# Turning v by VectorE in 32x32 blocks instead of by TensorE, in a channel attention with a gated convolution

## Chip, core and metric

The kernel runs on one core of a Trainium2 chip. The metric is the device time of one execution in microseconds (us); the median of the runs counts. The engines are TensorE (PE; PEld is its weight load), VectorE (DVE), ScalarE (ACT), GpSimd (POOL) and SyncE (SP). SP and ACT issue the transfers, which 16 DMA queues carry.

## The reference

Four batches (B = 4) of q, k, v with N = 6336 rows and C = 256 channels, float32. The attention is over channels: the scores are a 256x256 matrix, summed over all rows.

```python
qn = q / (np.linalg.norm(q, axis=1, keepdims=True) + 1e-06)
kn = k / (np.linalg.norm(k, axis=1, keepdims=True) + 1e-06)
s = kn.transpose(0, 2, 1) @ qn / tau
a = softmax(s, axis=-1)                  # 256 x 256 a batch
x = v @ a                                # 6336 x 256
gate_pre[t] = sum over k of conv_w[k] * x[t - 4 + k]   # 5 taps, causal, per channel
out = (sigmoid(gate_pre) * (x @ w_val)) @ w_out
```

## The kernel before

**Scores.** q and k come in groups of three rows a partition (`load_group`, tile `raw`, six buffers). `score_group` splits them into a high part in a reduced format (`hi`, ACT cast, L196) and the rest (POOL subtraction, L197), and TensorE adds three products of the parts into `s_ps` (L232). In the first batch most groups go in unsplit. For the norms ACT squares (`sq`, L213), and DVE and POOL add the squares (`acc_ps` and `acc`, L218).

**Softmax.** `softmax(b)` is a generator. Each `tick()` issues its next piece, between pieces of other work. At its end the batch has its weights `w` (a, and a times w_val, both split).

**The gated convolution.** The rows are cut into 13 chunks a batch: 12 of 508 rows and one of 240, each with a halo of 4 rows ahead of it. The products need v with channels on the partitions. So `load_v` brings a chunk with rows on the partitions (`v_raw`, three buffers), and `transpose_v` turns it: eight TensorE transposes of 128x128 a chunk into PSUM (`t_ps`, L359), an ACT cast to `v_hi` (L360), and a DVE subtraction to `v_lo` (L361), for each half of the channels. `product` makes x (`x_ps`) and x times w_val (`val_ps`) at L369, `conv` sums the five taps (ACT at L383, DVE at L385), `sigmoid`, `value` (DVE, L398) and `split_g` (`g_hi` on ACT, L411; `g_lo` on POOL, L412) follow, and `finish` multiplies by w_out (L428) and stores.

**The order.** The last loop runs over the 52 chunks of all batches. Chunk n's step holds sigmoid, value and split of n, the convolution of n + 1, the transposes of n + 2, the load of n + 3, the product with w_out of n - 1, and one or two groups of the next batch's scores, until they run out. In the first batch nothing but scores can run. A scheduler then places each instruction on its engine's queue by its own estimate of times. `behind(...)` adds that what follows is placed after a marked instruction. Each engine runs its queue in order.

Of the kernel before, what the change touches and what calls it, by code (L numbers as in the profile page):

```python
# [9 lines left out]
F32 = mybir.dt.float32  # L10
F32R = mybir.dt.float32r
# [3 lines left out]
ALU = mybir.AluOpType  # L15
# [3 lines left out]
P = 128  # L19
GROUP = 3  # L20
LEAD = 4
PREFETCH = 4
VLEAD = 2
SIDE, LAST = 5, 15
HALO = 4
ROWS = 508
# [3 lines left out]
def kernel(  # L30
# [13 lines left out]
    nc = tc.nc  # L44
    B, N, C = q.shape
    K = conv_w.shape[0]
    NH = C // P
# [4 lines left out]
    raw_p = ctx.enter_context(tc.tile_pool(name="raw_p", bufs=6))  # L52
# [4 lines left out]
    v_p = ctx.enter_context(tc.tile_pool(name="v_p", bufs=VLEAD + 1))  # L57
    w_p = ctx.enter_context(tc.tile_pool(name="w_p", bufs=2))
    ps_s = ctx.enter_context(tc.tile_pool(name="ps_s", bufs=1, space=PSUM))
    ps = ctx.enter_context(tc.tile_pool(name="ps", bufs=4, space=PSUM))  # L60
# [23 lines left out]
    ident = const.tile([P, P], F32, name="ident")  # L84
# [245 lines left out]
    NT = -(-(HALO + WMAX) // P)  # L330

    vraw, vt = {}, {}

    def load_v(b, i):

        t0, w = chunks[i]
        t = raw_p.tile([P, NT, C], F32, name="v_raw", bufs=3)
        j0 = 0
        if i == 0:
            nc.gpsimd.memset(t[0:HALO, 0, :], 0.0)  # L340
            nc.sync.dma_start(out=t[HALO:P, 0, :], in_=v[b, 0:P - HALO])
            j0 = 1
        full, rest = divmod(HALO + w, P)
        lo = t0 - HALO
        nc.sync.dma_start(out=t[:, j0:full, :], in_=v[b, lo + j0 * P:lo + full * P].rearrange("(j p) c -> p j c", p=P))
        if rest:
            nc.sync.dma_start(out=t[0:rest, full, :], in_=v[b, lo + full * P:t0 + w])
        vraw[b, i] = t

    def transpose_v(b, i, h):  # L350
        w = HALO + chunks[i][1]
        if h == 0:
            vt[b, i] = [v_p.tile([P, NH, HALO + WMAX], F32R, name=name) for name in ("v_hi", "v_lo")]
        th, tl = vt[b, i]
        src = vraw[b, i]
        tp = ps.tile([P, 512], F32, name="t_ps", tag="bank")
        for j in range(-(-w // P)):
            np_ = min(P, w - j * P)
            marks["PE"] = nc.tensor.transpose(tp[:, j * P:j * P + np_], src[0:np_, j, h * P:(h + 1) * P], ident[0:np_, 0:np_])  # L359
        nc.scalar.copy(th[:, h, 0:w], tp[:, 0:w])  # L360
        nc.vector.tensor_tensor(tl[:, h, 0:w], tp[:, 0:w], th[:, h, 0:w].bitcast(F32), ALU.subtract)  # L361

    def product(ps, wt, which, b, i, h, lo, hi_):
        th, tl = vt[b, i]
        hs = slice(h * P, (h + 1) * P)
        n_ = 0
        for ch in range(NH):
            for ws, vs in ((0, th), (0, tl), (1, th)):
                marks["PRODUCT"] = nc.tensor.matmul(ps, wt[:, which, ws, ch, hs], vs[:, ch, lo:hi_], start=n_ == 0, stop=n_ == 3 * NH - 1)  # L369
                n_ += 1  # L370
# [86 lines left out]
    @contextmanager  # L457
    def behind(*engines):
        with ExitStack() as st:
            for e in engines:  # L460
                st.enter_context(tc.issue_after(marks[e].ins))
            yield
# [34 lines left out]
    def step(n):  # L497
        return all_steps[n] if 0 <= n < len(all_steps) else None
# [24 lines left out]
        for _ in gen:  # L523
            pass
    tick()
    with tc.high_priority(), behind("PE", "ACT"):
        for h in range(NH):
            transpose_v(*step(0), h)
    with behind("PE", "ACT"):
        run_group()  # L530
    with behind("PE"):
# [16 lines left out]
    if WORDS == 2:  # L548
        with behind("ACT"):
            nc.scalar.copy(wo_hi.rearrange("p h e -> p (h e)"), w_raw["out"][:, :, 1].bitcast(F32))  # L550
    for h in range(NH):
        transpose_v(*step(1), h)
    with behind("ACT"):
        split_group()

# [6 lines left out]
    for n in range(len(all_steps)):  # L562
# [32 lines left out]
                with behind("ACT"):  # L595
                    split_group()
        if new:
            for h in range(NH):
                transpose_v(*new, h)
        tick()  # L600
        if prev:
            with behind(*{len(all_steps) - 2: ["CONV"], len(all_steps) - 1: ["G"]}.get(n, [])):
# [34 lines left out]
```

## Time and profile before

| | |
|---|---|
| median of 3 runs | 655.57 us (655.3 to 656.13) |
| profiled execution, span from first to last instruction | 653.5 us |
| mean granted TensorE clock | 0.998 |
| transposes `t_ps` on TensorE | 400 of 416 recorded, 54.2 us modelled busy time for the full ones |
| bytes from HBM, to HBM | 79.11 MB, 25.95 MB |

The span begins with the first instruction and ends with the last. The median is of executions without the profiler, which take a little more than the span from end to end. A row of the profile has line, engine, operation, tiles, shapes and count, then the busy time and the mean of one instruction, then the idle time ahead of them and what ended it.

### The profile page before, as it was taken

To read this page: it belongs to the slowest core of one execution; us is meant where nothing else is said; L and a number is where in the kernel's file an instruction comes from. 1 tells how busy PE (TensorE), PEld (TensorE's weight loads), DVE (VectorE), ACT (ScalarE), POOL (GpSimd) and SP (SyncE) were. 2 spreads that over 40 slices of the span, in tenths; PEclk is the share of its full clock that TensorE was granted. 3 is DMA by queue.
4 is the path that set the end of the run, shared out by engine and by line. 5 is a ranking of instruction groups with operands and counts; after the bars stand their busy time and mean duration, and the time that the engine had idled before them with its cause. 6 is when DMAs were issued, how large, how long until landed. Compare 5 with 4: busy or idle time off the path is not lost.

```text
span 653.5 us, 10735 instructions
## 1 busy us (share of the span) xinstructions
PE 638.5 (98%) x4040; PEld 572.4 (88%) x4040; DVE 509.2 (78%) x831; ACT 466.8 (71%) x612; POOL 372.7 (57%) x181
## 2 busy tenths in 40 slices
PE   8899899999999999999999999999999899999996
PEld 7788699999989999998998999999989798888886
DVE  3694788887858787777877788887777879888884
ACT  4466978768688886777679887686877755655564
POOL 2591787949645786767855489496763122212221
PEclk9999999999999999999999999999999999999999
DMA  8999864646545564555645366453322343343213
GB/s 259 331 329 346 265 211 144 196 135 193 151 135 163 182 206 136 187 162 156 190 143 159 122 220 192 158 181 96 88 63 87 99 123 106 110 130 106 63 48 104
DMA packets 107876, 105.77 MB, mean 162 GB/s; under 512 B 5744, under 2 KB 107312, under 8 KB 107824
## 3 DMA queue, kind: packets, MB, share of 16 engines
q1 hardware_dynamic: 82048, 79.76, 39.6%
q10 hardware_dynamic: 25776, 25.32, 12.3%
q8 instruction: 32, 0.52, 0.3%
q14 instruction: 20, 0.16, 0.1%
HBM read 79.11 MB, written 25.95 MB: 161 GB/s over the span
## 4 chain that ended last, share of the span: by engine, by line
PE 87%; ACT 5%; SPq 3%; POOL 2%; issue 1%; DMA 1%; DVE 0%; ACTq 0%
PE o_ps L428 21%; PE x_ps L369 20%; PE val_ps L369 19%; PE s_ps L232 19%; PE t_ps L359 6%; SPq L75 2%; POOL hi L197 2%; DMA raw<-in_k_dram 1%; PE o_ps L318 1%; ACT hi L196 1%; ACT sq L213 1%; ACT L391 1%; ACT s L292 0%; SPq L125 0%; SPq L120 0%
## 5 line engine op out<-in xcount | busy, mean ns | idle before, releaser
L385 DVE SCALAR_TENSOR_TENSOR gate<-x_ps,wa,gate 128x508 f32<-128x508 f32 (+1 forms) x416 | 273.9, 716 | 15.8 <-ACT gate L383 14.9
L197 POOL TENSOR_TENSOR hi<-raw,hi 128x1536 fp32r<-128x1536 f32 (+2 forms) x51 | 166.1, 3259 | 103.2 <-ACT hi L196 103.2
L412 POOL TENSOR_TENSOR g_lo<-gate,g_hi 128x1016 fp32r<-128x1016 f32 (+1 forms) x50 | 117.5, 2351 | 125.9 <-ACT g_hi L411 125.8
L218 DVE TENSOR_TENSOR acc_ps<-acc_ps,sq 128x512 f32<-128x512 f32 (+1 forms) x124 | 86.5, 698 | 81.2 <-ACT sq L213 79.3
L369 PE MATMUL x_ps<-v_hi,w 128*128 128x512 f32 (+1 forms) x416 | 138.6, 392 | 0.5 <-DVE gate L385 0.3
L369 PE MATMUL val_ps<-v_hi,w 128*128 128x508 f32 (+1 forms) x416 | 134.1, 382 | 0.6 <-DVE w L323 0.5
L232 PE MATMUL s_ps<-hi 128*128 128x256 f32 (+1 forms) x846 | 119.6, 286 | 2.8 <-POOL hi L197 2.8
L232 PEld LDWEIGHTS s_ps<-hi 128*128 128x128 f32 (+1 forms) x846 | 109.6, 190 | 7.1 <-POOL hi L197 3.6
L428 PE MATMUL o_ps<-wo_hi,g_hi 128*128 128x256 f32 x400 | 112.9, 282 | 1.4 <-ACT at L313 1.4
L438 ACT COPY o_sb<-o_ps 128x512 f32<-128x512 f32 x99 | 58.2, 590 | 76.8 <-PE o_ps L428 76.6
L428 PE MATMUL o_ps<-wo_lo,g_hi 128*128 128x256 f32 x400 | 112.3, 281 | 0.0
L428 PE MATMUL o_ps<-wo_hi,g_lo 128*128 128x256 f32 x400 | 112.0, 280 | 0.0
L218 POOL TENSOR_TENSOR acc<-acc,sq 128x512 f32<-128x512 f32 x68 | 88.1, 1296 | 36.8 <-ACT sq L213 35.7
L213 ACT ACTIVATE sq<-raw 128x1536 f32<-128x1536 f32 (+3 forms) x69 | 95.9, 1393 | 15.8 <-DMA raw<-in_k_dram 10.4
L369 PEld LDWEIGHTS x_ps<-v_hi,w 128*128 128x128 f32 x416 | 77.4, 188 | 16.1 <-DVE gate L385 1.7
L369 PEld LDWEIGHTS val_ps<-v_hi,w 128*128 128x128 f32 x416 | 77.1, 188 | 14.4 <-DVE w L323 1.0
L383 ACT ACTIVATE gate<-x_ps,wa 128x508 f32<-128x508 f32 (+1 forms) x104 | 68.1, 669 | 18.8 <-PE x_ps L369 18.1
L398 DVE TENSOR_TENSOR gate<-val_ps,gate 128x508 f32<-128x508 f32 (+1 forms) x104 | 64.3, 657 | 21.7 <-ACT gate L391 20.0
L369 PE MATMUL x_ps<-v_lo,w 128*128 128x512 f32 (+1 forms) x208 | 79.6, 383 | 0.0
L369 PE MATMUL val_ps<-v_lo,w 128*128 128x508 f32 (+1 forms) x208 | 79.0, 380 | 0.0
L360 ACT CAST v_hi<-t_ps 128x512 fp32r<-128x512 f32 (+1 forms) x104 | 55.5, 570 | 32.9 <-PE t_ps L359 32.9
L428 PEld LDWEIGHTS o_ps<-wo_hi,g_hi 128*128 128x128 f32 x400 | 75.3, 188 | 2.3 <-ACT at L313 1.6
(80 smaller groups left out, 800.3 us busy)
## 6 DMA issues: line engine op xcount, KB each, us to landing
raw<-in_q_dram SPq DMA_DIRECT2D x64, 384.0 KB
raw<-in_k_dram SPq DMA_DIRECT2D x64, 384.0 KB
v_raw<-in_v_dram SPq DMA_DIRECT2D x44, 512.0 KB
out_dram<-o_sb ACTq DMA_DIRECT2D x47, 384.0 KB
out_dram<-o_sb ACTq DMA_DIRECT2D x47, 124.0 KB
v_raw<-in_v_dram SPq DMA_DIRECT2D x4, 384.0 KB
raw<-in_q_dram SPq DMA_DIRECT2D x4, 128.0 KB
raw<-in_k_dram SPq DMA_DIRECT2D x4, 128.0 KB
```

The source lines that it names most:

```text
L197: nc.gpsimd.tensor_tensor(hi[r, js, :, 1, :], raw[r, js, :, :], hi[r, js, :, 0, :].bitcast(F32), ALU.subtract)
L213: nc.scalar.activation(sq[0:np_, ja:jb], raw[0:np_, ja:jb], AF.Square)
L218: add = eng.tensor_tensor(st[key][0:np_], st[key][0:np_], sq[0:np_, j], ALU.add)
L232: marks["PE"] = nc.tensor.matmul(st["s"][:, h, :], lhs, rhs, start=False, stop=stop and h == NH - 1 and n_ == len(ops) - 1)
L360: nc.scalar.copy(th[:, h, 0:w], tp[:, 0:w])
L369: marks["PRODUCT"] = nc.tensor.matmul(ps, wt[:, which, ws, ch, hs], vs[:, ch, lo:hi_], start=n_ == 0, stop=n_ == 3 * NH - 1)
L383: nc.scalar.activation(gate[:, h, 0:w], x_ps[:, 0:w], AF.Copy, scale=cw[:, h, 0:1])
L385: nc.vector.scalar_tensor_tensor(gate[:, h, 0:w], x_ps[:, tap:tap + w], cw[:, h, tap:tap + 1], gate[:, h, 0:w], ALU.mult, ALU.add)
L398: nc.vector.tensor_tensor(gate[:, h, 0:w], val_ps[:, 0:w], gate[:, h, 0:w], ALU.mult)
L412: nc.gpsimd.tensor_tensor(gl[:, :, 0:w], gate[:, :, 0:w], gh[:, :, 0:w].bitcast(F32), ALU.subtract)
L428: nc.tensor.matmul(o_ps[:, u * C:(u + 1) * C], gs[:, h, off:off + P], ws[:, h, :], start=n_ == 0, stop=n_ == 3 * NH - 1)
L438: marks["ACT"] = nc.scalar.copy(o_sb[:, j:j + len(pair), :], o_ps[:, 0:len(pair) * C].rearrange("p (j c) -> p j c", c=C))
```

## The change

A chunk is loaded so that 32x32 blocks are enough to turn it. For each of the four quadrants of 32 partitions and each half of the channels one transfer brings 32 channels of all rows of the chunk: row r of each group of 32 rows goes to partition r of the quadrant. Turning each 32x32 block in place on VectorE then puts channel c on partition c, and rows along the free dimension. Both channel halves lie in one tile, so ScalarE casts a whole chunk with one instruction, and the subtraction, one a chunk too, goes to GpSimd. The widths are rounded up to 32 (512 and 256 columns; the narrow chunk begins some rows earlier, and `span_v` gives the offset).

```diff
+Q = 32
+    VW = -(-(HALO + WMAX) // Q) * Q
+    def span_v(i):
+        t0, w = chunks[i]
+        cols = -(-(HALO + w) // Q) * Q
+        base = min(t0 - HALO, N - cols)
+        return base, cols, t0 - HALO - base
     def load_v(b, i):
-        t0, w = chunks[i]
-        t = raw_p.tile([P, NT, C], F32, name="v_raw", bufs=3)
-        j0 = 0
-        if i == 0:
-            nc.gpsimd.memset(t[0:HALO, 0, :], 0.0)
-            nc.sync.dma_start(out=t[HALO:P, 0, :], in_=v[b, 0:P - HALO])
-            j0 = 1
-        full, rest = divmod(HALO + w, P)
-        lo = t0 - HALO
-        nc.sync.dma_start(out=t[:, j0:full, :], in_=v[b, lo + j0 * P:lo + full * P].rearrange("(j p) c -> p j c", p=P))
-        if rest:
-            nc.sync.dma_start(out=t[0:rest, full, :], in_=v[b, lo + full * P:t0 + w])
+        base, cols, _ = span_v(i)
+        g = cols // Q
+        t = raw_p.tile([P, NH, VW // Q, Q], F32, name="v_raw", bufs=3)
+        for j in range(P // Q):
+            part = t[j * Q:(j + 1) * Q]
+            if base < 0:
+                nc.gpsimd.memset(part[0:-base, :, 0, :], 0.0)
+            for h in range(NH):
+                c0 = h * P + j * Q
+                g0 = 0
+                if base < 0:
+                    nc.sync.dma_start(out=part[-base:Q, h, 0, :], in_=v[b, 0:Q + base, c0:c0 + Q])
+                    g0 = 1
+                nc.sync.dma_start(out=part[:, h, g0:g, :],
+                                  in_=v[b, base + g0 * Q:base + cols, c0:c0 + Q].rearrange("(g r) q -> r g q", r=Q))
-    def transpose_v(b, i, h):
-        ...
-        for j in range(-(-w // P)):
-            np_ = min(P, w - j * P)
-            marks["PE"] = nc.tensor.transpose(tp[:, j * P:j * P + np_], src[0:np_, j, h * P:(h + 1) * P], ident[0:np_, 0:np_])
-        nc.scalar.copy(th[:, h, 0:w], tp[:, 0:w])
-        nc.vector.tensor_tensor(tl[:, h, 0:w], tp[:, 0:w], th[:, h, 0:w].bitcast(F32), ALU.subtract)
+    def transpose_v(b, i):
+        g = span_v(i)[1] // Q
+        th, tl = vt[b, i] = [v_p.tile([P, NH, VW // Q, Q], F32R, name=name) for name in ("v_hi", "v_lo")]
+        t = vraw.pop((b, i))
+        for h in range(NH):
+            nc.vector.transpose(t[:, h, 0:g, :], t[:, h, 0:g, :])
+        marks["V"] = nc.scalar.copy(th[:, :, 0:g, :], t[:, :, 0:g, :])
+        nc.gpsimd.tensor_tensor(tl[:, :, 0:g, :], t[:, :, 0:g, :], th[:, :, 0:g, :].bitcast(F32), ALU.subtract)
     ...
-    with tc.high_priority(), behind("PE", "ACT"):
-        for h in range(NH):
-            transpose_v(*step(0), h)
+    with tc.high_priority(), behind("ACT"):
+        transpose_v(*step(0))
```

`product` takes its columns at the offset of `span_v`. The scheduler makes a new order out of this. Three places matter below. The names end in running numbers of the buffers.

On POOL, in the middle of the second batch's scores, two steps read before:

```order
L412 TENSOR_TENSOR g_lo_1205<-gate_1010,g_hi_1204 128x1016
L197 TENSOR_TENSOR hi_1278<-raw_874,hi_1278 128x6x256
L218 TENSOR_TENSOR acc_455<-acc_455,sq_1279 128x512
L412 TENSOR_TENSOR g_lo_1329<-gate_1163,g_hi_1328 128x1016
L197 TENSOR_TENSOR hi_1404<-raw_998,hi_1404 128x6x256
L218 TENSOR_TENSOR acc_455<-acc_455,sq_1405 128x512
```

and now, at the same place (lines have moved by up to 10):

```order
L369 TENSOR_TENSOR v_lo_1215<-v_raw_980,v_hi_1214 128x1024
L422 TENSOR_TENSOR g_lo_1061<-gate_898,g_hi_1060 128x1016
L198 TENSOR_TENSOR hi_1160<-raw_765,hi_1160 128x6x256
L219 TENSOR_TENSOR acc_476<-acc_476,sq_1161 128x512
L369 TENSOR_TENSOR v_lo_1336<-v_raw_1130,v_hi_1335 128x1024
L198 TENSOR_TENSOR hi_1281<-raw_886,hi_1281 128x6x256
L219 TENSOR_TENSOR acc_476<-acc_476,sq_1282 128x512
L422 TENSOR_TENSOR g_lo_1211<-gate_1019,g_hi_1210 128x1016
```

One `v_lo` a chunk has come in, ahead of that step's `hi` or `g_lo`.

On DVE, in the first batch's softmax (`s` the scores, `m` their extremes, `rz` the inverse sums), before:

```order
L276 TENSOR_SCALAR nk_475<-o_ps_465,rtau_107 128x2
L218 TENSOR_TENSOR acc_ps_454<-acc_ps_454,sq_490 128x512
L287 SCALAR_TENSOR_TENSOR s_432<-s_432,nk_475,o_ps_465 128x256 x2
L289 TENSOR_REDUCE m_485<-s_432 128x2
L294 TENSOR_SCALAR o_ps_465<-o_ps_465 128x2
L296 RECIPROCAL rz_505<-o_ps_465 128x2
```

and now:

```order
L277 TENSOR_SCALAR nk_496<-o_ps_486,rtau_107 128x2
L367 STREAM_TRANSPOSE v_raw_379<-v_raw_379 128x512 x2
L219 TENSOR_TENSOR acc_ps_475<-acc_ps_475,sq_511 128x512
L288 SCALAR_TENSOR_TENSOR s_463<-s_463,nk_496,o_ps_486 128x256 x2
L290 TENSOR_REDUCE m_506<-s_463 128x2
L367 STREAM_TRANSPOSE v_raw_388<-v_raw_388 128x512 x2
L295 TENSOR_SCALAR o_ps_486<-o_ps_486 128x2
L297 RECIPROCAL rz_526<-o_ps_486 128x2
```

The block transposes of chunks 1 and 2 stand inside the softmax; chunk 0's stand ahead of it.

On SP, after the first batch's last group, before:

```order
L341 DMA v_raw_352<-in_v_dram 124x256
L345 DMA v_raw_352<-in_v_dram 128x3x256
L75 DMA raw_356<-in_q_dram 128x3x256
L75 DMA raw_356<-in_k_dram 128x3x256
L75 DMA raw_359<-in_q_dram 128x3x256
L75 DMA raw_359<-in_k_dram 128x3x256
L345 DMA v_raw_362<-in_v_dram 128x4x256
L345 DMA v_raw_364<-in_v_dram 128x4x256
```

and now, from the last of the sixteen transfers of chunk 0 on:

```order
L358 DMA v_raw_352<-in_v_dram 32x15x32
L76 DMA raw_373<-in_q_dram 128x3x256
L76 DMA raw_373<-in_k_dram 128x3x256
L76 DMA raw_376<-in_q_dram 128x3x256
L76 DMA raw_376<-in_k_dram 128x3x256
L358 DMA v_raw_379<-in_v_dram 32x16x32 x8
L358 DMA v_raw_388<-in_v_dram 32x16x32 x8
L76 DMA raw_440<-in_q_dram 128x3x256
```

The groups of the second batch stand behind 32 transfers of v instead of 4.

More of the change, by code (lines that the diff above doesn't have):

```diff
@@ L350, in transpose_v @@
-    def transpose_v(b, i, h):
[L351 to L356, printed above, removed]
-        for j in range(-(-w // P)):
-            np_ = min(P, w - j * P)
-            marks["PE"] = nc.tensor.transpose(tp[:, j * P:j * P + np_], src[0:np_, j, h * P:(h + 1) * P], ident[0:np_, 0:np_])
-        nc.scalar.copy(th[:, h, 0:w], tp[:, 0:w])
-        nc.vector.tensor_tensor(tl[:, h, 0:w], tp[:, 0:w], th[:, h, 0:w].bitcast(F32), ALU.subtract)
+    VW = -(-(HALO + WMAX) // Q) * Q
@@ L363, in product @@
+    def transpose_v(b, i):
[6 more added lines that the diff above has]
+        nc.gpsimd.tensor_tensor(tl[:, :, 0:g, :], t[:, :, 0:g, :], th[:, :, 0:g, :].bitcast(F32), ALU.subtract)
     def product(ps, wt, which, b, i, h, lo, hi_):
-        th, tl = vt[b, i]
+        th, tl = (t.rearrange("p h g q -> p h (g q)") for t in vt[b, i])
+        at = span_v(i)[2]
+        lo, hi_ = at + lo, at + hi_
@@ L550 @@
             nc.scalar.copy(wo_hi.rearrange("p h e -> p (h e)"), w_raw["out"][:, :, 1].bitcast(F32))
-    for h in range(NH):
-        transpose_v(*step(1), h)
+    transpose_v(*step(1))
     with behind("ACT"):
@@ L597 @@
         if new:
-            for h in range(NH):
-                transpose_v(*new, h)
+            transpose_v(*new)
         tick()
```

## The prediction

> **What bounds the kernel now.** I read the page first: its totals, the busy slices and the chain that ended last.
>
> ```profile
> span 653.5 us, 10735 instructions
> PE 638.5 (98%) x4040; PEld 572.4 (88%) x4040; DVE 509.2 (78%) x831; ACT 466.8 (71%) x612; POOL 372.7 (57%) x181
> DMA  8999864646545564555645366453322343343213
> PE 87%; ACT 5%; SPq 3%; POOL 2%; issue 1%; DMA 1%; DVE 0%; ACTq 0%
> PE o_ps L428 21%; PE x_ps L369 20%; PE val_ps L369 19%; PE s_ps L232 19%; PE t_ps L359 6%; SPq L75 2%; POOL hi L197 2%; DMA raw<-in_k_dram 1%; PE o_ps L318 1%; ACT hi L196 1%; ACT sq L213 1%; ACT L391 1%; ACT s L292 0%; SPq L125 0%; SPq L120 0%
> ```
>
> TensorE carries 87% of the chain, and the transposes that the change removes are 6% of it. A modelled busy share isn't proof of a full engine, so I looked at the chain in order of time late in the run, where only the gated convolution is left:
>
> ```profile
> 574.06 0.87 PE t_ps L359 x8
> 574.93 2.75 PE x_ps L369 x12
> 577.69 2.82 PE o_ps L428 x24
> 580.51 2.74 PE val_ps L369 x12
> 583.25 0.87 PE t_ps L359 x8
> ```
>
> Each piece starts where the one before ends: 0.87 + 2.75 + 2.82 + 2.74 = 9.18 us, and the next chunk starts 9.19 us after this one. TensorE truly sets the step, and 0.87 us of it are transposes. Then the stages, one row each (the columns: length; PE, PEld, DVE, ACT, POOL busy; clock; DMA share; GB/s), and the transposes alone in the same stages:
>
> ```profile
> core 0: us, PE busy (x) PEld busy (x) DVE busy (x) ACT busy (x) POOL busy (x), PEclk, DMA share, GB/s
> 53.00:80.00 27.00, 24.39 (x126) 19.54 (x125) 16.09 (x30) 21.91 (x34) 12.52 (x8) 1.00 0.96 303
> 80.00:182.00 102.00, 102.00 (x680) 92.98 (x678) 85.04 (x131) 76.60 (x93) 77.73 (x34) 1.00 0.56 173
> 200.00:338.00 138.00, 138.00 (x924) 126.26 (x923) 111.80 (x179) 105.15 (x130) 99.47 (x43) 1.00 0.55 170
> 358.00:503.00 145.00, 145.00 (x968) 132.58 (x967) 115.11 (x186) 110.75 (x140) 98.85 (x43) 1.00 0.43 133
> 523.00:640.00 117.00, 116.98 (x732) 104.50 (x730) 99.76 (x157) 68.68 (x106) 30.21 (x13) 1.00 0.32 99
> ...
> 80.00:182.00 102.00, 10.31 (x72) 8.71 (x72) 1.00 0.56 173
> 200.00:338.00 138.00, 12.46 (x92) 10.77 (x92) 1.00 0.55 170
> 358.00:503.00 145.00, 13.08 (x97) 11.40 (x98) 1.00 0.43 133
> 523.00:640.00 117.00, 12.92 (x100) 11.27 (x97) 1.00 0.32 99
> ```
>
> Eight transposes are one chunk of v, so these stages hold 72/8 = 9, 11.5, 12.1 and 12.5 chunks. In the three mixed stages (scores of the next batch beside this batch's convolution) POOL is 76%, 72% and 68% busy; in the last stage DVE is at 85%.
>
> **What the change removes.** 416 transposes on TensorE, none added. The most this can give is the 6.2% that t_ps holds of the chain, 0.062 x 653.5 = 40.5 us. By stage, at 0.87 us a chunk: 7.8, 10.0, 10.5 and 10.9 us. Those are floors for TensorE of 94.2, 128.0, 134.5 and 106.1 us.
>
> **What it moves to GpSimd, ScalarE and VectorE.** The nearest rows:
>
> ```profile
> L412 POOL TENSOR_TENSOR g_lo<-gate,g_hi 128x1016 fp32r<-128x1016 f32 x47 | 113.8, 2422 | 121.6 <-ACT g_hi L411 121.5
> L361 DVE TENSOR_TENSOR v_lo<-t_ps,v_hi 128x512 fp32r<-128x512 f32 x96 | 62.8, 681 | 9.3 <-ACT v_hi L360 9.3
> L360 ACT CAST v_hi<-t_ps 128x512 fp32r<-128x512 f32 x96 | 52.8, 587 | 30.6 <-PE t_ps L359 30.6
> L411 ACT CAST g_hi<-gate 128x1016 fp32r<-128x1016 f32 x47 | 49.2, 1047 | 2.1 <-DVE gate L398 2.0
> L89 DVE MEMSET zeros<- 128x512 f32 x1 | 0.5, 485 | 0.1
> L151 DVE TENSOR_SCALAR w_raw<-w_raw 128x512 int32<-128x512 int32 x2 | 2.5, 1256 | 0.0
> ```
>
> *POOL* gets one subtraction of 128x1024 for each chunk. Its twin is g_lo, 2422 ns at 1016 columns, so 2.44 us. That is the dearest item: 52 chunks add about 122 us to 372.7. By stage POOL then holds 77.73 + 9 x 2.44 = 99.7, 99.47 + 28.1 = 127.5, 98.85 + 29.6 = 128.4, and 30.2 + 30.5 = 60.7 us. Against TensorE's floors (94.2, 128.0, 134.5) POOL is over in the first mixed stage and level in the second. So POOL becomes the co-bound there, and it can't be packed perfectly: in-order, it waits for ScalarE's casts. How full it gets is unknown, so I bound it:
>
> ```profile
> 275.00:287.00 12.00, 12.00 (x81) 10.97 (x81) 10.68 (x17) 8.80 (x12) 11.10 (x6) 1.00 0.55 170
> ```
>
> Here it reached 11.10/12 = 92.5% without stopping TensorE; the other end is 100%. I take 96%, the middle. Stage times are the larger of POOL/0.96 and TensorE's floor: 103.9 (+1.9), 132.8 (-5.2) and 134.5 against POOL's 133.8 (-10.5): -13.8 in all. At 92.5% they are 107.8, 137.8, 138.8: -0.6. At 100%: 99.7, 128.0, 134.5: -22.8.
>
> *DVE* loses two subtractions for each chunk (681 ns) and gains two block transposes of 128x512. No row shows one. Between the memset (485) and the slowest row of this width (1256) I take 681, the width's usual price: no change. Then DVE holds 99.8 us of TensorE's 106.1 in the last stage, 94%; I give that stage -9 of its -10.9. With 485 the stage gets its -10.9; with 1256 it has 25 x 0.575 = 14.4 us more, 114.2, and -3. The Trainium skill (Vector Engine (DVE) Microarchitecture Reference, The reshape front-end and per-opcode configuration) says the transpose sustains one element per cycle per lane; no run yet shows it.
>
> *ACT* trades two casts (2 x 587) for one of about 1047 ns: nothing, ScalarE being at 76% at most.
>
> **The loads.** 60 transfers of 1 KB rows become 448 (8 a chunk, 8 more for each batch's first) of 128-byte rows.
>
> ```profile
> q1 hardware_dynamic: 82048, 79.76, 39.6%
> q10 hardware_dynamic: 25776, 25.32, 12.3%
> ...
> DMA packets 600, 0.07 MB, mean 180 GB/s; under 512 B 565, under 2 KB 569, under 8 KB 600
> q1 hardware_dynamic: 600, 0.07, 123.1%
> ...
> DMA packets 91, 0.16 MB, mean 402 GB/s; under 512 B 2, under 2 KB 23, under 8 KB 91
> q1 hardware_dynamic: 91, 0.16, 106.9%
> ```
>
> SP's packets take 0.396 x 16 x 653.5 us / 82048 = 50.5 ns, nearly all of 1 KB. The last two pairs are stretches of 0.4 us, at 14.2 us and 15.0 us, when the weights came in. At 14.2 us: 0.4 x 16 x 1.069 = 6.84 us, less 21 packets of 1 KB, leaves 85 ns for each of 68 packets of 2 KB. At 15.0 us 565 are the 8-byte words of conv_w and semaphore writes: 7.88 us less 31 x 0.085 and 4 x 0.05 leaves 8.9 ns each. 128 bytes lie near the small end: 8.9 + 41.6 x 120/1016 = 13.8, so 14 ns; bounds 8.9 and 50.5. Wide chunks need 16 x 32 x 8 = 4096 packets, narrow ones half: 204,800 x 14/16 = 179 us of all 16 queues, where 25,536 x 50.5/16 = 81 stood. The mean share goes from 52% to about 67%: hidden in the mixed stages, at 56% now. At 50.5 ns it would not be (below).
>
> SP issues more, too:
>
> ```profile
> L345 SPq DMA_DIRECT2D v_raw<-in_v_dram x52: 340/368/975, 44.9 to 602.5; - x52
> SPq L345 <- PE t_ps L359: 298.5, 44, 14.7
> 61.12 0.88 DVE s L287 x2
> 63.99 0.18 DVE o_ps L294
> ```
>
> 8 x 0.37 = 3 us a chunk against 9 to 13 us for its step. The loads wait on their buffer for 298.5 us now: they go out as soon as it's free, chunks ahead, so a release after POOL's subtraction instead of the transpose costs nothing in the steady state. If that lead is gone, DVE's in-order transpose waits for the landing, and the gate work behind it.
>
> The start is different: chunks 0 to 2 load while the queues are at 96%, in 32 issues (8 more for chunk 0's zero rows are among them) in place of 4. In the new order two transposes stand ahead of L287's place in the softmax chain and two ahead of L294's, a ScalarE cast beside each pair. If the data is just there, 4 x 0.68 + 2 x 1.05 = 4.8 us enter the chain, less 0.87 of removed transposes: +4. Bounds: -1 (all hidden) and +10 (28 issues of 0.37 us ahead of it).
>
> **Sum.** -13.8 (mixed) - 9 (last stage) - 1 (one chunk at each of three batch turns, not all on the chain) + 4 (start) = -19.8: a span of 633.7 us. The median, 655.57, is 2.1 us over this execution's span, so 635.8 us.
>
> **The rivals.**
> *TensorE stays the only bound*: POOL and DVE fill to 100% and the start hides its loads. Then all 40.5 us go: 615 us. For it: the lead of several chunks. Against: POOL's 99.7 us in a stage that TensorE would leave at 94.2.
> *POOL eats it*: it fills to 92.5% and no more, DVE's transposes cost more than a subtraction: -0.6 - 5 - 1 + 4 = -2.6, at 653 us; between this and my case lie 645 to 654.
> *The packets of 128 bytes bound the kernel* (slower): place, the 16 queues in the start and the first mixed stage. Without v that stage uses 57.1 - 9 x 512 x 50.5/16 ns = 42.6 of 102 us; it is full, and the kernel gains nothing there, at 59.4 us / (9 x 4096) x 16 = 25.8 ns a packet. At 28 ns, twice my price: 107.1 (+5.1), 139.7 (+1.7), -10.5, -9, -1, and at the start 3 x (7.2 - 1.6) = +17: 659 us. At 50.5 ns the stages take 159, 206, 199 and 179 us: over 900. For it: no packet of this size is in the trace. Against: 8-byte packets at 8.9 ns. The Trainium skill (DMA: Bandwidth & Descriptors, Specifications) speaks for it: under 512 B a transfer is off line rate, since the engine reads, modifies and writes; it gives no price. Conv_w's packets here don't show one.
> That the transposes stay on TensorE is out: no row of the new order has them.
>
> **Chances.** My case (622 to 645): 0.50. TensorE alone (under 622): 0.12. POOL eats it (645 to 654.2): 0.16. Within 0.2%, about what can be told from no change here (654.3 to 656.9): 0.04. Slower: 0.18, of it 0.10 the packets and 0.08 in-order waits. So faster 0.78. The range 617 to 662 leaves out some 0.06 below and 0.10 above; it holds 92.5% and 100% for POOL, both ends of the DVE price, and packets up to 28 ns.
>
> **What would show it.** t_ps gone and TensorE's busy time some 40 us less; v_lo on POOL at 2.4 us, POOL above 93% in the first mixed stage, waits of s_ps or o_ps for POOL's hi or g_lo; block transposes near 0.68 us; a q1 share near 55%; DVE waiting for v's loads only at the start. The forecast is wrong if the small packets take over 25 ns, if the transposes take over 1.2 us, or if TensorE waits for v_lo itself.

## The result, and the profile after

The changed kernel takes 685.37 us (median of four runs, 682.22 to 686.64) beside 655.43 us for the kernel before in the same series: 1.0451 times as long, 95% interval 1.0427 to 1.0476. It is 30 us slower where the forecast was 20 us faster, and it lies outside the forecast range. The profiled execution took 686.16 us, its span 684.4 us. The page of the changed kernel, the rows that answer to those shown of before:

```profile
span 684.4 us, 10756 instructions
PE 617.3 (90%) x3640; PEld 544.3 (80%) x3640; DVE 512.7 (75%) x831; ACT 466.5 (68%) x560; POOL 490.3 (72%) x245
DMA  8987988765668587777666477754225445555212
PE 22%; DMA 20%; SPq 19%; POOL 16%; DVE 9%; issue 7%; ACT 7%; DVEq 0%; POOLq 0%; ACTq 0%
```

TensorE lost its 400 recorded transposes and 21 us of busy time, and its share of the chain fell from 87% to 22%. No other engine took over: loads, SP's queue and GpSimd hold 55% of the chain together. That is what a loop through several engines would look like. The stages of the changed kernel, in the columns of the prediction's table:

```profile
53.00:80.00 27.00, 16.31 (x62) 12.94 (x61) 11.60 (x22) 13.88 (x23) 13.00 (x8) 0.75 0.87 231
80.00:182.00 102.00, 90.60 (x554) 79.87 (x553) 79.95 (x122) 74.12 (x78) 87.11 (x38) 1.00 0.75 181
200.00:338.00 138.00, 134.41 (x858) 121.16 (x857) 113.66 (x188) 113.41 (x133) 125.52 (x56) 1.00 0.72 176
358.00:503.00 145.00, 131.73 (x820) 118.59 (x819) 107.08 (x175) 104.86 (x122) 118.08 (x51) 0.95 0.56 137
523.00:640.00 117.00, 106.92 (x585) 91.23 (x584) 94.27 (x155) 69.82 (x97) 52.55 (x23) 0.96 0.47 100
```

In the first mixed stage nothing is full: TensorE 90.6 of 102 us, GpSimd 87.1, VectorE 80.0, the queues 75%. The third mixed stage looks alike. In the second TensorE is busy for 134.4 of 138 us, and there the kernel doesn't fall further behind (see the table below). The groups of the moved work, and four rows of the waits:

```profile
L369 POOL TENSOR_TENSOR v_lo<-v_raw,v_hi 128x1024 fp32r<-128x1024 f32 x48 | 115.8, 2411 | 24.9 <-ACT v_hi L368 19.9 <-DMA v_raw<-in_v_dram 4.5 <-DMA out_dram<-o_sb 0.4
L367 DVE STREAM_TRANSPOSE v_raw<-v_raw 128x512 f32<-128x512 f32 x96 | 66.1, 700 | 60.9 <-DMA v_raw<-in_v_dram 52.0 <-issue 4.4 <-DMA raw<-in_k_dram 2.2
L368 ACT CAST v_hi<-v_raw 128x1024 fp32r<-128x1024 f32 x48 | 50.3, 1048 | 30.8 <-PE val_ps L379 21.0 <-DVE v_raw L367 5.2 <-DMA v_raw<-in_v_dram 4.5
...
POOL g_lo L422 <- ACT g_hi L421: 81.4, 21, 7.4
DVE v_raw L367 <- DMA v_raw<-in_v_dram: 53.3, 31, 5.7
...
SPq L358 <- POOL v_lo L369: 138.7, 35, 18.4
SPq L76 <- POOL hi L198: 43.9, 19, 3.7
```

The durations of the moved instructions came out as forecast: 2411 ns for GpSimd's subtraction (2.44 us foretold), 700 ns for a block transpose (681), 1048 ns for the cast (1047). What the forecast did not count on is the second row of the waits: VectorE stands 53.3 us, 31 times, at block transposes whose v has not landed. The third says why it has not: SP's next load waits for GpSimd's `v_lo`. The chain in order of time shows the loop once round, at the turn from the first batch to the second:

```profile
219.91 2.35 POOL v_lo L369
222.28 0.33 SPq L358
...
224.77 0.49 SPq L358
225.26 0.04 issue
225.30 3.14 DMA v_raw<-in_v_dram
228.44 1.17 issue
229.61 0.10 DVE v_raw L367
...
230.25 0.71 DVE gate L395
230.95 0.62 DVE v_raw L367
231.57 1.28 DVE gate L395 x2
...
244.88 2.37 POOL v_lo L369
```

GpSimd's subtraction frees the load's buffer, SP issues eight transfers one after the other (most 0.49 us long), the last lands 3 us later, and VectorE, idle for 1.17 us at the transpose, turns the chunk and goes on with the *gate* work of a chunk that was turned long before. By this chain the next `v_lo` comes after work that this gate feeds.

Where the 30 us arise is seen from the start of each chunk's sigmoid, this kernel's less that of the kernel before (us, my reading of the traces; the kernels of the other rows come below):

```
chunk                          0     4    16    24    36    44    51
changed kernel              11.5  20.4  12.4  14.0  29.7  35.4  30.7
before, loads in 8 pieces   11.2  13.0  12.7  12.7  12.7  12.7  13.0
whole rows                   4.5   4.0  -2.0   1.8  -3.9   1.0   0.6
256-byte pieces              7.6   9.0   1.0   1.1   6.8  12.1  13.2
128-byte pieces, own tile   11.2  15.5  15.0  15.8   7.6   8.5   6.0
256-byte pieces, own tile    6.4  12.4   6.0   5.7  -0.1   0.5  -3.8
whole rows, own tile         6.1  12.1   5.9   6.3   0.1   1.5  -2.7
256, own tile, q and k first 6.8  11.3   1.6   0.4  -5.2  -5.6  -8.4
before, one turn of four     0.9  -0.5  -6.3  -8.2 -15.3 -20.4 -23.9
```

The changed kernel is 12 us late at the first chunk and 20 at the fifth, wins some of it back in the middle, loses 21 us between chunks 24 and 44, and gains 5 at the end, where there are no loads left.

### The profile page after: what moved, and what is told of

It is laid out like the page before. It is cut to its first block, busy times and chain, and to the rows that moved or that the text cites. A ratio compares the mean times of both kernels' runs of the same rounds, so it can differ in the third digit from the quotient of the medians.

```text
span 684.4 us, 10756 instructions
## 1 busy us (share of the span) xinstructions
PE 617.3 (90%) x3640; PEld 544.3 (80%) x3640; DVE 512.7 (75%) x831; ACT 466.5 (68%) x560; POOL 490.3 (72%) x245
## 3 DMA queue, kind: packets, MB, share of 16 engines
q1 hardware_dynamic: 267424, 79.83, 50.2%
## 4 chain that ended last, share of the span: by engine, by line
PE 22%; DMA 20%; SPq 19%; POOL 16%; DVE 9%; issue 7%; ACT 7%; DVEq 0%; POOLq 0%; ACTq 0%
SPq L358 14%; DMA v_raw<-in_v_dram 12%; PE o_ps L438 7%; POOL v_lo L369 7%; PE x_ps L379 6%; PE val_ps L379 5%; DVE gate L395 5%; DMA raw<-in_k_dram 4%; SPq L76 4%; DMA out_dram<-o_sb 4%; POOL hi L198 3%; POOL acc L219 3%; POOL g_lo L422 2%; PE s_ps L233 2%; ACT hi L197 2%
## 5 line engine op out<-in xcount | busy, mean ns | idle before, releaser
L395 DVE SCALAR_TENSOR_TENSOR gate<-x_ps,wa,gate 128x508 f32<-128x508 f32 (+1 forms) x416 | 281.2, 713 | 23.2 <-ACT gate L393 20.3
L379 PE MATMUL x_ps<-v_hi,w 128*128 128x512 f32 (+1 forms) x416 | 144.4, 398 | 27.1 <-DVE gate L395 21.8
L369 POOL TENSOR_TENSOR v_lo<-v_raw,v_hi 128x1024 fp32r<-128x1024 f32 (+1 forms) x52 | 120.9, 2325 | 36.9 <-ACT v_hi L368 31.9
L233 PE MATMUL s_ps<-hi 128*128 128x256 f32 (+1 forms) x846 | 115.9, 284 | 7.7 <-POOL hi L198 7.7
L219 DVE TENSOR_TENSOR acc_ps<-acc_ps,sq 128x512 f32<-128x512 f32 (+1 forms) x124 | 85.8, 692 | 45.6 <-ACT sq L214 43.4
L367 DVE STREAM_TRANSPOSE v_raw<-v_raw 128x512 f32<-128x512 f32 (+1 forms) x104 | 69.5, 680 | 65.5 <-DMA v_raw<-in_v_dram 53.3
L379 PEld LDWEIGHTS x_ps<-v_hi,w 128*128 128x128 f32 x416 | 80.3, 195 | 45.4 <-issue 16.1
L438 PE MATMUL o_ps<-wo_hi,g_lo 128*128 128x256 f32 x400 | 109.1, 288 | 6.2 <-POOL g_lo L422 6.1
L219 POOL TENSOR_TENSOR acc<-acc,sq 128x512 f32<-128x512 f32 x68 | 88.4, 1299 | 23.6 <-ACT sq L214 22.4
L393 ACT ACTIVATE gate<-x_ps,wa 128x508 f32<-128x508 f32 (+1 forms) x104 | 67.4, 664 | 36.3 <-PE x_ps L379 29.6
L379 PEld LDWEIGHTS val_ps<-v_hi,w 128*128 128x128 f32 x416 | 77.9, 190 | 15.7 <-ACT w L323 1.1
L401 ACT ACTIVATE gate<-gate 128x1016 f32<-128x1016 f32 (+1 forms) x52 | 52.9, 1018 | 48.9 <-DVE gate L395 48.4
L438 PEld LDWEIGHTS o_ps<-wo_hi,g_lo 128*128 128x128 f32 x400 | 74.5, 193 | 10.3 <-POOL g_lo L422 8.7
L379 PE MATMUL x_ps<-v_lo,w 128*128 128x512 f32 (+1 forms) x208 | 81.8, 393 | 0.0
```

The source lines that it names most:

```text
L219: add = eng.tensor_tensor(st[key][0:np_], st[key][0:np_], sq[0:np_, j], ALU.add)
L233: marks["PE"] = nc.tensor.matmul(st["s"][:, h, :], lhs, rhs, start=False, stop=stop and h == NH - 1 and n_ == len(ops) - 1)
L367: nc.vector.transpose(t[:, h, 0:g, :], t[:, h, 0:g, :])
L369: nc.gpsimd.tensor_tensor(tl[:, :, 0:g, :], t[:, :, 0:g, :], th[:, :, 0:g, :].bitcast(F32), ALU.subtract)
L393: nc.scalar.activation(gate[:, h, 0:w], x_ps[:, 0:w], AF.Copy, scale=cw[:, h, 0:1])
L395: nc.vector.scalar_tensor_tensor(gate[:, h, 0:w], x_ps[:, tap:tap + w], cw[:, h, tap:tap + 1], gate[:, h, 0:w], ALU.mult, ALU.add)
```

## The experiments

Ratios are to the kernel before on the same chip, with 95% intervals.

**1. The loads alone** (`b_pieces`: before, 8 pieces a chunk; TensorE turns as ever).

```
+ for c0 in range(0, C, 32):
+     nc.sync.dma_start(out=t[:, j0:full, c0:c0 + 32], in_=v[b, ..., c0:c0 + 32]...)
```

> The kernel before (TensorE turns v) with its loads cut into 8 pieces of 32 channels, 128-byte rows, as many packets and issues as in the changed kernel; the output is the same. Theory A (VectorE's in-order queue waits for loads that come just in time, because its block transposes stand 4 to 5 chunks ahead of their use): only the start pays, for 32 issues in place of 4; 658 to 668 us, and no new waits after the first batch. Rival B (GpSimd is overloaded): no GpSimd work is added here, so 655 to 668 as well. Rival C (204,800 small packets slow every load): the mixed stages pay too, 675 us or more.

667.79 us, 1.0196 (1.0181 to 1.0211), inside the range that theories A and B share; C falls. All of it is lost by the fifth chunk and none later, though the queues carry the same small packets to the end. So with TensorE turning v the pieces cost nothing in the steady state, as the forecast had it; at the start they cost 13 us.

**2. Whole rows** (`a_whole_rows`: the changed kernel, one transfer of 1 KB rows a chunk; the values then lie in other partitions, so the output is another).

> The changed kernel with a chunk loaded by one transfer of whole 1 KB rows; the block transposes, cast and subtraction are the same, but what is turned is not v in the right layout, so the output is another one. Theory A: the loads land in time, VectorE's waits for v (53 us) go, and so does the loss at the start; 630 to 645 us. Rival B: GpSimd has as much to do as before, 670 us or more. Rival C: 630 to 645 as well.

653.53 us, 0.9976 (0.9946 to 1.0006). The pieces are worth 32 us of the changed kernel, yet without them there is still no gain: the result lies between the two expected ranges, and no theory holds as it stands. VectorE still waits 41.5 us for v, with a single issue a chunk, so the wait does not need small pieces.

**3. and 4. VectorE's order** (`a_late`: block transposes queued behind the value product; `a_bufs`: 5 load buffers in place of 3).

```
+ marks["VAL"] = nc.vector.tensor_tensor(gate[:, h, 0:w], val_ps[:, 0:w], gate[:, h, 0:w], ALU.mult)
+ with behind("VAL"):
      transpose_v(*new)
```
```
- t = raw_p.tile([P, NH, VW // Q, Q], F32, name="v_raw", bufs=3)
+ t = raw_p.tile([P, NH, VW // Q, Q], F32, name="v_raw", bufs=5)
```

> The changed kernel with one edge more: the block transposes of chunk n+2 are queued behind the last value product of chunk n on VectorE, one chunk ahead of their use, where the new order had them 4 to 5 ahead. Loads, packets and all work are the same. Theory A: the waits of VectorE for v go after the start, 640 to 655 us (the start's loss of about 12 us stays). Rival B: 675 us or more, GpSimd has the same work. Rival C: 675 or more, the packets are the same.

> The changed kernel with 5 buffers for v's raw chunks in place of 3. The order then has the transposes 7 to 8 chunks ahead of their use, again right behind the loads. Theory A: the distance from landing to transpose stays as short, so 675 to 695 us. Rival D (too few buffers, the loads start too late): 635 to 655 us. B and C: no change.

717.63 us, 1.0954 (1.0933 to 1.0976), and 721.94 us, 1.1033 (1.1001 to 1.1065): both far slower. The first refutes theory A's 640 to 655 us; it lies in the "675 us or more" of B and C, which had expected no gain but gave no reason for a loss of 32 us. The second is outside every range. In `a_late` VectorE's wait for v is down to 9.7 us, as meant. Two of its waits:

```profile
DVE acc_ps L219 <- ACT sq L214: 94.9, 47, 5.6
...
PE o_ps L438 <- POOL g_lo L422: 29.6, 27, 2.0
```

VectorE's 94.9 us stood at 43.4 in the changed kernel, but at 79.3 in the kernel before, where they cost nothing, so this wait alone explains little. TensorE's wait for `g_lo` is more to the point: 29.6 us, against 6.1 in the changed kernel. Why `a_late` is so slow stays open. In `a_bufs` the planner, given more buffers, put the transposes 7 chunks ahead of the value product (median, my count), where they had stood 5 ahead, and VectorE waited 64.2 us for v. So neither "later" nor "earlier" is a cure by itself.

**5. and 6. No turning at all** (`b_no_turn`: before without its transposes, casts and VectorE's subtractions reading v from SBUF; `a_no_turn`: experiment 2 without block transposes. In both v is used unturned, so the outputs are others).

> The kernel before without its 416 transposes: ScalarE's casts and VectorE's subtractions read the raw chunk as it lies, so the output is another one. Nothing is put in their place. Theory E (TensorE bounds the kernel before, what is lost comes later, from GpSimd and the loads): all 40 us go, 613 to 623 us. Theory F (the other engines are near their own limits in the order that the scheduler makes, so that TensorE's time can't be taken out): 630 to 650 us.

> The changed kernel with whole-row loads (653.5 us) and without the block transposes on VectorE; one cast and one subtraction on GpSimd a chunk remain. The output is another one. Theory E, with GpSimd as the cause: GpSimd has the same work, 645 to 656 us. Theory A (VectorE's in-order waits for v in front of its block transposes are the loss that is left): 615 to 635 us.

668.27 us, 1.0205 (1.019 to 1.022), and 637.84 us, 0.9735 (0.9707 to 0.9762). The first was slower with 40 us of TensorE work taken out, which no theory had. One group had changed its duration, and all that had changed in it was an operand's place (681 ns with PSUM before):

```profile
L358 DVE TENSOR_TENSOR v_lo<-v_raw,v_hi 128x512 fp32r<-128x512 f32 x96 | 127.4, 1347 | 2.6 <-ACT v_hi L357 2.4
```

So it was no test of the transposes. The timeline of VectorE and GpSimd shows what happens (three rows, both engines):

```profile
213.82 2.68 DVE L358 TENSOR_TENSOR v_lo<-v_raw,v_hi 128x512 fp32r<-128x512 f32 x1
217.08 0.68 DVE L358 TENSOR_TENSOR v_lo<-v_raw,v_hi 128x512 fp32r<-128x512 f32 x1
...
213.55 2.40 POOL L409 TENSOR_TENSOR g_lo<-gate,g_hi 128x1016 fp32r<-128x1016 f32 x1
```

The subtraction that starts 0.27 us into GpSimd's `g_lo` ends 0.55 us after it (216.50 against 215.95 us); the next one, with GpSimd idle, takes 0.68 us. By my count over the trace, 57 of the 96 start while a GpSimd instruction runs, and 54 of these end 546 to 555 ns after that instruction does (the other three 584 to 651); the 38 that touch none take 672 to 693 ns. With a PSUM source (before) 45 lie wholly inside a GpSimd instruction and still take 677 to 692 ns. The Trainium skill (SBUF — State Buffer, Who interferes with whom) says that a VectorE instruction with two SBUF inputs contends with a GpSimd instruction that reads SBUF, and that the ports they share are locked by one of them at a time. The trace agrees, at 1347 against 681 ns in the mean.

`a_no_turn` lies between the two expected ranges, 15.7 us under experiment 2. Its load buffer is still freed only by GpSimd's subtraction, but the first reader is ScalarE's cast, which comes 26.3 us after SP's last issue of the chunk (median): with whole rows, a late release alone does not make the kernel slow.

**7. The subtraction back on VectorE** (`a_vlo_dve`).

```
- nc.gpsimd.tensor_tensor(tl[:, :, 0:g, :], t[:, :, 0:g, :], th[:, :, 0:g, :].bitcast(F32), ALU.subtract)
+ nc.vector.tensor_tensor(tl[:, :, 0:g, :], t[:, :, 0:g, :], th[:, :, 0:g, :].bitcast(F32), ALU.subtract)
```

> The changed kernel (685 us) with the subtraction to v_lo on VectorE instead of GpSimd; loads and block transposes stay. Theory E, with GpSimd as the cause: the mixed stages lose their waits for hi and g_lo, 655 to 670 us. Theory A: the loads still come just in time ahead of the transposes, 678 to 695 us.

765.71 us, 1.1687 (1.1668 to 1.1707), slower than both expected. The same contention shows at twice the width: 1856 ns in the mean for 1024 columns, where those without a GpSimd instruction beside them (18, my count) take 1181 to 1227. It makes some 31 us of the 89 that VectorE got (48 x 0.64 us); how the 80 us of loss divide was not separated. Giving the subtraction to GpSimd was no mistake of the change, once v is turned in SBUF.

**8. 256-byte pieces** (`a_256`: channels split into even and odd, so that a quadrant's two halves lie side by side; 4 transfers a chunk).

> The changed kernel with even channels in one half and odd ones in the other, so that a quadrant takes 64 neighbouring channels: 4 transfers a chunk with 256-byte rows instead of 8 with 128-byte rows, half the packets and issues. The columns of k are taken with step 2 to match, and the output is the same. If the pieces are what costs (32 us between the changed kernel and the one with whole rows): the start loses about 7 us in place of 12, and the later waits for v halve; 662 to 672 us. If it is the in-order places alone: 680 us or more.

663.87 us, 1.0145 (1.0111 to 1.018): expected if the pieces cost, and 21.5 us better than the changed kernel.

**9. One transpose of four** (`b_one_turn`): experiment 5 with the operands left in PSUM (the turned block is used four times over, so the output is another).

```
- for j in range(-(-w // P)):
-     marks["PE"] = nc.tensor.transpose(tp[:, j * P:j * P + np_], ...)
+ marks["PE"] = nc.tensor.transpose(tp[:, 0:P], src[:, 0, h * P:(h + 1) * P], ident)
```

> The kernel before with one PE transpose of four: each half of a chunk turns its first 128 positions alone, and ScalarE's cast and VectorE's subtraction read that PSUM block four times over (so the output is another; both keep a PSUM source and their 512 columns). TensorE loses 304 of its 416 transposes, some 30 us of the 6.2% that the chain of waits gave them, and no operand moves to SBUF. Theory E (the kernel before is bound by TensorE, and the 668 us of the kernel without any transpose came from its subtraction, which took 1347 ns with both operands in SBUF against 681 ns from PSUM): 622 to 632. Theory F (the planned order and the loops of waits take most of what TensorE gives up): 640 to 652.

631.6 us, 0.9622 (0.9606 to 0.9639), inside the range of theory E. 304 transposes are worth 24.7 us, 83% of the 29.6 us that their share of the chain stood for (304/416 of 40.5), and by the table the gain grows evenly to the end. TensorE's transposes were worth removing.

**10. Number or size of the transfers** (`a_rows_8`: 8 transfers a chunk, of 64 whole rows each).

> The changed kernel with 1 KB rows (whole rows of v) in 8 transfers a chunk of 64 rows each, in place of 8 of 512 pieces of 128 bytes (the values in the partitions are other ones, so the output is another). Bytes and number of transfers are those of the changed kernel, the packet is 8 times as large. Theory S (the number of transfers costs: SP's 0.49 us for each and 8 transfers in flight, so that one chunk fills the queue): 670 to 690, the start as late as in the changed kernel (+9 to +12 us at the first chunk). Theory P (the packet size costs): 650 to 662, like the 653.5 us with one transfer a chunk, the start +4 to +7.

666.19 us, 1.0151 (1.0115 to 1.0187): between the two, 13 us above one transfer a chunk and 19 below the changed kernel. Both seem to count in the kernels that turn in place. How the 32 us divide exactly stays open, since the three kernels' plans also differ in VectorE's order.

**11. and 12. The buffer freed early** (`a_outplace`, and `a_256_out` on experiment 8).

```
+ rows = vraw.pop((b, i))
+ t = raw_p.tile([P, NH, VW // Q, Q], F32, name="v_t", bufs=2)
- nc.vector.transpose(t[:, h, 0:g, :], t[:, h, 0:g, :])
+ nc.vector.transpose(t[:, h, 0:g, :], rows[:, h, 0:g, :])
```

> The changed kernel with the block transposes written to a tile of their own (2 buffers), so that a load's buffer is free as soon as VectorE has turned it, and GpSimd's subtraction no longer holds up the loads. Theory L (the loop GpSimd v_lo, SP's 8 issues, landing, transpose is the loss in the mixed stages): 650 to 668, SP's waits for v_lo gone. Theory D (VectorE's order is the loss: it stands at transposes that the plan puts 3 to 5 chunks ahead): 680 to 700, with VectorE's wait for v's transfers at 50 us or more.

> The kernel with 256-byte pieces (4 transfers a chunk) and the block transposes written to a tile of their own, 2 buffers. Theory L: both gains add, 632 to 648, which would beat the kernel before. Theory D: 660 to 672, no better than the 663.9 us of 256-byte pieces turned in place.

661.73 us, 1.0082 (1.0057 to 1.0108): 23.6 us back, with no other edit than the place of the result, inside the range of theory L. 651.91 us, 0.9939 (0.9917 to 0.9961): 0.6% under the kernel before, though 4 us short of the expectation. The waits of `a_outplace`, SP's and VectorE's:

```profile
SPq L358 <- DVE v_t L368: 150.6, 35, 10.5
...
DVE v_t L368 <- DMA v_raw<-in_v_dram: 13.3, 6, 5.5
```

SP still waits as long, but for VectorE's transpose, one step after the landing, instead of GpSimd's `v_lo`; and VectorE waits 13.3 us in place of 53.3. The two buffers also bind the plan: a transpose can't be placed more than two chunks ahead of the `v_lo` that frees its tile, and it now stands 4 chunks ahead of the value product in place of 5. Which of the two matters, the early release or the later turn, was not separated.

**13. Whole rows, buffer freed early** (`a_whole_out`; other values in the partitions, as in 2).

> The changed kernel with one whole-row transfer of 1 KB rows a chunk and block transposes into a tile of their own, 2 buffers (the values in the partitions are other ones, so the output is another). What remains of the loss then is neither transfers nor the load's buffer. If the transfers still cost in the kernel with 256-byte pieces (651.9 us): 636 to 645. If they no longer do, and VectorE's and GpSimd's work is what is left: 647 to 653.

651.33 us, 0.9936 (0.9919 to 0.9954), like the 651.91 us with four 256-byte pieces and as the second expectation had it. With the result in a tile of its own, 256-byte pieces cost nothing that shows, and those of 128 bytes 10 us (661.73). But against experiment 2 the own tile gains only 2.2 us here: by the table 8 us are lost by the fifth chunk and 11 won after it.

**14. The subtraction from PSUM** (`a_256_psum`: block transposes write a PSUM bank; VectorE subtracts).

```
+ turned = ps.tile([P, VW // Q, Q], F32, name="v_t", tag="bank")[:, 0:g, :]
+ nc.vector.transpose(turned, rows[:, h])
+ nc.vector.tensor_tensor(tl[:, h, 0:g, :], turned, th[:, h, 0:g, :].bitcast(F32), ALU.subtract)
```

> 256-byte pieces; VectorE's block transposes write into a PSUM bank, from which ScalarE casts and VectorE subtracts (681 ns with a PSUM source), half by half; GpSimd has no v_lo. If GpSimd's 2.4 us a chunk is what is left of the loss against the 624 us or so that a TensorE without transposes would allow: 632 to 646. If VectorE becomes the bound instead (512.7 us busy + 104 x 0.68 us = 583 us, and its order stands at loads): 655 to 680.

691.85 us, 1.0565 (1.0543 to 1.0588), above even the slow range. The group is quick again, beside GpSimd's work and all:

```profile
L373 DVE TENSOR_TENSOR v_lo<-v_t,v_hi 128x512 fp32r<-128x512 f32 x96 | 64.5, 683 | 0.6 <-ACT v_hi L372 0.3
```

So the contention hangs on the second SBUF operand. But taking the work from GpSimd won nothing: VectorE is busy 565.8 us now, and TensorE's output products wait 18.1 us for its `v_lo`. They don't read `v_lo`; both use the PSUM buffers of tag `bank`, so this is probably a wait for a buffer. The run doesn't tell VectorE's load from that of the banks.

**15. and 16. The first softmax's order** (`a_start`, and `a_256_start` on experiment 12): transposes of chunks 1 and 2 behind the softmax's reciprocal on VectorE.

```
+ marks["RZ"] = nc.vector.reciprocal(rz, z)
+ with behind("RZ"):
      transpose_v(*step(1))
```

> The changed kernel with the block transposes of chunks 1 and 2 placed behind the softmax steps of the first batch on VectorE (behind the reciprocal of L297); nothing else is moved. Theory Q (the first chunk is late because VectorE stood 5.73 us at chunk 1's transposes, before the softmax's L288, which came at 67.4 us against 61.1): the first sigmoid 4 to 7 us earlier, and 676 to 682 in all. Theory R (the loads themselves are late: 32 issues of SP and small packets, chunk 0's cast and the next q and k loads behind them): the first sigmoid within 2 us of the changed kernel, 682 to 688.

> The kernel with 256-byte pieces and the block transposes in a tile of their own (651.9 us), with the transposes of chunks 1 and 2 behind the first batch's softmax steps on VectorE as well. Theory Q: the first sigmoid 4 to 6 us earlier, 645 to 648. Theory R: 650 to 654. Under both it stands below the kernel before.

685.43 us, 1.0432 (1.0387 to 1.0477), and 653.2 us, 0.9964 (0.9951 to 0.9977). Theory Q falls: in `a_256_start` L291, the softmax step that was L287 before, ran at 61.16 us (61.12 before), but the first sigmoid of `a_start` came at 93.04 us, in the changed kernel at 93.12. Something else that had become late shows in the start of the changed kernel, in SP's queue and TensorE's:

```profile
54.05 0.49 SPq L76 DMA_DIRECT2D raw<-in_k_dram  x1
55.06 0.37 SPq L76 DMA_DIRECT2D raw<-in_q_dram  x1
55.48 0.47 SPq L76 DMA_DIRECT2D raw<-in_k_dram  x1
56.01 12.23 SPq L358 DMA_DIRECT2D v_raw<-in_v_dram  x16
68.35 0.42 SPq L76 DMA_DIRECT2D raw<-in_q_dram  x1
...
63.07 2.76 PE L233 MATMUL s_ps<-raw 128*128 128x256 f32 x12
73.49 5.32 PE L233 MATMUL s_ps<-raw 128*128 128x256 f32 x12 [7.66 <-DMA raw<-in_k_dram]
```

and in the kernel before:

```profile
49.45 1.27 SPq L345 DMA_DIRECT2D v_raw<-in_v_dram  x2
50.83 2.50 SPq L75 DMA_DIRECT2D raw<-in_q_dram  x1
```

The q and k loads that follow chunks 1 and 2 are issued at 68.35 us instead of 50.83. TensorE, in order, stands 7.66 us at the second batch's scores with the first batch's products behind them. Its granted clock in 53 to 80 us is 0.75 instead of 1.00, and twelve score matmuls take 5.32 us where they took 2.76 ten microseconds earlier. Over the runs, clock and delay go together: with 1.00 in this stretch the first sigmoid is 0.9 to 4.5 us late, with 0.87 it is 6.1 to 7.3, with 0.75 to 0.81 it is 7.6 to 12.6. Which makes which is not shown.

**17. and 18. q and k first** (`a_kfirst`, and `a_256_kfirst` on experiment 12).

```
- load_upto(NG + 3)
+ load_upto(NG + 5)
```

> The changed kernel with the loads of v's chunks 1 and 2 (16 issues) behind two more groups of q and k loads at the start (load_upto NG + 5 in place of NG + 3); nothing else is moved. Theory K (the first chunk is late because TensorE stands at the next batch's scores, whose k load waited behind v's issues in SP's queue): the first sigmoid 5 to 9 us earlier than in the changed kernel, 674 to 680 in all if the later loops keep the gain. If it is not K: the first sigmoid within 2 us, 682 to 688.

> The kernel with 256-byte pieces and block transposes into a tile of their own (651.9 us), with the same move of the loads of chunks 1 and 2. Theory K: the first sigmoid 3 to 6 us earlier, 645 to 650 in all. If it is not K, or the later loops take the gain back: 651 to 655.

648.02 us, 0.9889 (0.9865 to 0.9912), with 256-byte pieces: the fastest kernel of this study that turns v, 1.1% under the kernel before. With 128-byte pieces turned in place 703.98 us, 1.074 (1.0718 to 1.0761). In `a_kfirst` TensorE's wait for k is gone:

```profile
64.98 5.35 PE L233 MATMUL s_ps<-raw 128*128 128x256 f32 x24
```

24 score matmuls run without a stop and at full rate, and the first sigmoid is 2.6 us earlier (90.56 us), between the 5 to 9 of theory K and the 2 of its opposite; the total is outside both ranges. So the wait for k accounts for a small part of the start's loss. `a_kfirst` then lost far more in the steady state: one chunk took 28 us, with GpSimd idle for 12.7 us at `v_lo` and SP behind it. The plan had moved with the loads. The total of `a_256_kfirst` is in theory K's range, but not by its mechanism: `a_256_out` had no wait of that kind to lose (1.7 us for k in the whole run), and the first sigmoid comes at 88.36 us instead of 88.02. Most of the gain arises between chunks 4 and 16, and no run tells why.

## Why the prediction was wrong

**The step that failed** is the sentence on the loads: "so a release after POOL's subtraction instead of the transpose costs nothing in the steady state". The lead that it rests on was there: in the kernel before, TensorE turned a chunk 32.8 us after SP's last issue for it. The changed kernel does not keep it (medians over the chunks from the fourth on, my reading of the traces; then VectorE's wait for v and the kernel's time):

```
                              last issue   VectorE waits   time,
                              to turn, us     for v, us     us
before                            32.8             -      655.43
before, 8 pieces (1)              27.3             -      667.79
changed kernel                     1.4          53.3      685.37
whole rows (2)                     4.6          41.5      653.53
transposes late (3)               23.0           9.7      717.63
5 buffers (4)                      2.1          64.2      721.94
256-byte pieces (8)                4.3          38.6      663.87
own tile (11)                     24.4          13.3      661.73
256, own tile (12)                28.9           6.5      651.91
whole rows, own tile (13)         31.1           5.8      651.33
```

VectorE turns a chunk 5 chunks ahead of its value product (median), where TensorE turned it 1 ahead. So the lead now lies behind the turn: VectorE stands in its order at the landing, the turned chunk then lies in the load's buffer for 20.5 us until GpSimd's `v_lo`, and the next load goes out only after that. The prediction names this case ("if that lead is gone, DVE's in-order transpose waits for the landing, and the gate work behind it") and gave it 0.08, without asking whether the later release and the new order would take the lead away. With a tile of its own for the result the lead is back, and the kernel is 23.6, 12.0 and 2.2 us faster (11 against the changed kernel, 12 against 8, 13 against 2). The lead alone doesn't set the time, though: `a_late` has it and is slow, and with whole rows the kernel does without it.

**The start** was put at +4 us, with bounds -1 and +10. It was +11.5 at the first chunk. The bound of 10 us counted SP's issues ahead of v. The issues also delay the q and k loads behind them, for which TensorE waits; the order showed those groups "behind 32 transfers of v instead of 4", and I priced only the softmax. That wait gave back 2.6 us of the 11.5 (17), and the softmax steps nothing (15, 16). What makes the rest stays open.

**TensorE's 40.5 us** were sound: 24.7 us for 304 of 416 transposes (9). The rival that only TensorE bounds the kernel was right about the kernel before.

**GpSimd** was rightly priced (2411 ns) and rightly named as TensorE's co-bound in the mixed stages. In `a_256_kfirst` it is 96.67 of 102 us busy in the first mixed stage, 95%, near the 96% that I took. The lag there falls from 11.3 at chunk 4 to -5.2 at chunk 36, 16.5 us where the sum had 13.8. The total came near, but by luck: the sum had +1.9, -5.2 and -10.5 for the three batches, and the lag fell by 6.3 (chunks 4 to 12), 6.3 (13 to 25) and 2.9 (26 to 38). In the changed kernel GpSimd never filled in the first mixed stage (87.11 of 102).

**The last stage** was put at -9 and gave -3.2 there (from -5.2 at chunk 36 to -8.4) and -3.7 in `a_256_out` (from -0.1 to -3.8). What limits it was not separated.

**The block transposes** took 700 ns, 681 being taken. The Trainium skill (Vector Engine (DVE) Microarchitecture Reference, The reshape front-end and per-opcode configuration) gives the transpose a rate of one element per cycle per lane; 700 ns beside the 681 of a subtraction of the same width fit a rate near that of an elementwise pass.

**The packets** took 12.9 ns in the mean, read by size in the trace (204,672 packets of 128 bytes); 14 was taken. SP's queue has 50.2% of the 16 queues, where the prediction looked for 55%. The rival that the packets bound the kernel is out, by this and by experiment 1; its side of the result came true by another mechanism.

Step by step for the version with 256-byte pieces, an own tile, and q and k first: start +11.3 by the fifth chunk (foretold +4), mixed stages -16.5 (-13.8), last stage -3.2 (-9): -8.4 us at the last sigmoid, where the forecast had -19.8.

**What stays open.** The same instructions, turned in place and with 128-byte pieces, took 685, 685, 704 and 718 us in four plans (the changed kernel, `a_start`, `a_kfirst`, `a_late`). Differences of 19 us and more between in-place kernels can thus be a matter of the plan, and the shares of packet size and transfer number (10) are no finer than that. The same holds for the size of the own tile's gain: that it comes from the load's buffer rests on three pairs, all of one sign, and on the waits and leads above. Whether the early release or the later turn brings it, and how the 30 us divide between the loop and the plan, no run separates.

## What to carry to other kernels

When a step is moved to another engine, ask what its old place released, and when. A load that seems chunks ahead is so only because its buffer is freed early; if the last reader becomes an engine with little time to spare, and an in-order engine consumes the next load, the lead can turn into a wait for everything queued behind it. Writing the result to a tile of its own was worth 23.6 us here with the smallest pieces; larger pieces were worth as much or more (21.5 us with 256 bytes, 31.8 with whole rows), and the gains did not add up.

When a load is split into more transfers, list what stands behind it in the issuing queue, other streams' loads first, and look for the engine that waits for those.

## What the runs showed that was not expected

- VectorE's subtraction with both inputs in SBUF waits for GpSimd's running instruction: 1347 ns in the mean against 681 with one input in PSUM, and in one row 2.68 us against 0.68. A kernel without TensorE's transposes was 2% slower with it; with three of four transposes out and the operand left in PSUM it was 4% faster.
- A packet of 128 bytes is cheap in absolute terms and dear by the byte: 12.9 ns against 52.7 for 1 KB in the same trace, so 10 against 19 bytes a ns. The Trainium skill (DMA: Bandwidth & Descriptors, Specifications) puts transfers under 512 B off line rate; the trace agrees, by a factor of two at 128 bytes.
- More buffers made the kernel slower (five in place of three: 721.94 against 685.37 us). The plan then put the transposes 7 chunks ahead in place of 5, still at the landing (2.1 us after the last issue); that this is the reason is likely but not shown.
